# Rounding float64 weights to fp32: integer steps on ACT, DVE and GpSimd in place of identity products on PE

## The chip, the cores and the metric

The kernel runs on one core of a Trainium2 chip. Five instruction streams work side by side and meet only at semaphores: PE (matrix products), DVE (VectorE), ACT (ScalarE), POOL (GpSimd) and SP (which here only issues transfers). The metric is the device time of one execution in microseconds. The kernel before took 420.8 us in the median of three runs (420.77 to 421.42). A difference of about 0.2% (0.84 us) is what a measurement of this kernel can tell from no change.

## The reference

Per batch and head, 32 packed queries `p` attend over the keys and values, then the 576 queries `q` attend over the 32 packed rows. The result goes through a gated feed-forward layer. The three weights reach the kernel as float64; everything else is float32.

```python
def sm_attn(qq, kk, vv):
    s = scale * np.matmul(qq, kk.transpose(0, 1, 3, 2))
    s = s - np.max(s, axis=-1, keepdims=True)
    a = np.exp(s)
    a = a / (np.sum(a, axis=-1, keepdims=True) + 1e-09)
    return np.matmul(a, vv)
p_packed = sm_attn(p, k, v)            # 8 batches, 8 heads, 576 rows, 64 wide; 32 packed rows
x = sm_attn(q, p_packed, p_packed)     # then (8, 576, 512)
h = np.maximum(x @ w_in, 0.0)          # w_in 512 x 1024
conv_out += conv_w[k][None, None, :] * hp[:, k:k + S, :]   # 3 taps along the rows
gate = 1.0 / (1.0 + np.exp(-conv_out))
out = (h * gate @ w_out)               # w_out 1024 x 512
```

## The kernel before

The work is cut into sixteen attention groups (four heads of a batch each), eight batches of the feed-forward layer with eight column blocks j each, and 36 output tiles m of 128 rows.

- `attention(g)`: scores of the packed queries (PE L443), maximum and exponential (DVE L481, ACT L485), transposes on PE (L492) and copies out of PSUM on ACT (L495), the product with v (L501), then the second softmax on DVE (L525 to L555) with an exponential on ACT (L535).
- `packed_weight(b, hf)`: multiplies the packed values into half of `w_in` (L575), and splits the result into a high and a low part (ACT L587; the rest on DVE or on PE L591).
- `ffn1(b, j)`: twelve products in three part pairs (L627), ReLU and the middle tap on ACT (L639, L643), the other taps, a tanh and the gate (DVE L645, L649, L655, ACT L653). It writes one slice of `hgt`.
- `ffn2(m)`: splits an output tile's input into `xhi` (ACT L673) and `xlo` (DVE L676) and multiplies by `wo_hi` and `wo_lo` in 24 products (PE L692). The first of them, `ffn2(0)`, needs all eight slices of batch 0 and all four pieces of `w_out`. In the text its first product is called the **first output product**.
- `weight(i)`, i = 0 to 7: one megabyte of float64 weights each, four pieces of `w_in` and four of `w_out`. `f64_parts` turns the upper words into a truncated fp32 number (ACT L266, DVE L268, L270) and the lower words into a rest (DVE L272). PE adds the parts with products by an identity `ident` and its negative `minus` (L324), and ACT copies the sum out of PSUM (L328). For `w_out`, ACT also writes a high part `wo_hi` (L317), and the products give the rest.

The order of the instructions on each engine is a table, `ORDER`: two characters per step name the stream whose next step is issued. The class `Flow` carries a planner's costs along with it and puts filler products (`warm`, PE L242, products of `ident` with itself whose result nobody reads) into places where the planner sees PE idle, up to the first output product and not behind it. SP issues the transfers in the table's order through one queue; each `weight` loads into one of three buffers (`stage` and two parts of `hgt1`), which are reused once a piece has been read.

Of the kernel before, what the change touches and what calls it, by code (L numbers as in the profile page):

```python
# [49 lines left out]


# [11 lines left out]
class Flow:  # L63
# [10 lines left out]
    FILL_NS, FILL_COLS, MARGIN = 216, 512, 100  # L74

    LAG = {
        "PE": dict(PE=0, ACT=197, DVE=196, SP=200, POOL=200),
        "ACT": dict(PE=216, ACT=153, DVE=142, SP=200, POOL=200),
        "DVE": dict(PE=256, ACT=128, DVE=127, SP=200, POOL=200),
        "DATA": dict(PE=820, ACT=908, DVE=908, SP=0, POOL=0),  # L80
    }
# [103 lines left out]
def tile_packed_attention_conv_gate(  # L185
# [65 lines left out]
    def big():  # L251
        return ps.tile([128, 2, 512], F32, name="big", tag="big", bufs=3)
# [1 line left out]
    def small(tag="sm"):  # L254
        return ps.tile([128, 512], F32, name=tag, tag=tag)

    def f64_parts(tiles, raw, m, after=(), take=(), sets=None):

        pair = raw.rearrange("r (c t) -> r c t", t=2)
        up = pair[:, :, 1].bitcast(I32)  # L260
        low = pair[:, :, 0].bitcast(U32)
        yield Step("ACT", 93 + m * 14 // 15, after=after, take=take)
        t, e, rest = tiles()
        ti, ei = t.bitcast(I32), e.bitcast(I32)

        nc.scalar.activation(out=e, in_=up.bitcast(F32), func=AF.Prelu, scale=F64_REBIAS, alpha=-(2.0**32))  # L266
# [3 lines left out]
        nc.vector.tensor_scalar(out=ei, in0=ti, scalar1=-0x800000, scalar2=None, op0=ALU.bitwise_and)  # L270
        yield Step("DVE", 69 + m * 100 // 96, sets=sets)
        nc.vector.scalar_tensor_tensor(  # L272
            out=rest,
            in0=low,
            scalar=2.0**-52 if rest.dtype == F32 else -(2.0**-52),
            in1=e,
            op0=ALU.mult,
            op1=ALU.mult,
        )
# [17 lines left out]
    def weight(i):  # L297

        c, cols, src, st = weight_tile(i)
        hi, lo = (w[:, 2 * (i % 4) : 2 * (i % 4) + 2, :].rearrange("r c f -> r (c f)") for w in (wo_hi, wo_lo))  # L300
        token, tags = ("gw", ("ghi", "glo")) if i < 2 else ("x", ("xhi", "xlo"))
        parts = []

        def tiles():
            t, e = (wk.tile([128, DFF], F32, name="tmp", tag=tag) for tag in tags)
            parts.extend([(ident, t), (minus, lo)])
            return t, e, lo

        after = [("wd", i), "minus"] + ([("ws", i - 4)] if i >= 4 else [])
# [12 lines left out]
        for hf in range(2):
            for k, (w, x) in enumerate(parts):
                nc.tensor.matmul(  # L324
                    out=s[:, hf, :], lhsT=w, rhs=x[:, 512 * hf : 512 * hf + 512], start=k == 0, stop=k == len(parts) - 1
                )
        yield Step("ACT", 905, give=["big"], sets=[("w", i)])
        nc.scalar.copy(out=w_in_sb[:, c : c + 2, cols] if i < 4 else lo.rearrange("r (c f) -> r c f", c=2), in_=s)  # L328

    def conv_weight():  # L330
        src = conv_w.rearrange("k (j c) -> (k j) c", c=128)
# [1 line left out]
        st = [wk.tile([128, S], F32, name="s2", tag="s2") for _ in range(2)]  # L333
        if conv_w.dtype != F32:
            nc.gpsimd.dma_start(out=st[0][: 3 * NJ, :256].bitcast(I32), in_=src.bitcast(I32))
            t, e = st[1][: 3 * NJ, :128], st[1][: 3 * NJ, 128:256]
            yield from f64_parts(lambda: (t, e, e), st[0][: 3 * NJ, :256], 128)
            yield Step("DVE", 202)
            nc.vector.tensor_tensor(out=cw_raw, in0=t, in1=e, op=ALU.add)
# [414 lines left out]
```

## Time and profile before

| what | value |
|---|---|
| median of three runs | 420.8 us |
| span of the profiled execution | 418.8 us |
| what the runs have over the span | 2.0 us |
| PE instructions, DVE, ACT, POOL | 3343, 496, 440, 13 |
| HBM read and written | 37.77 MB, 9.44 MB |

The page gives the busy share of each engine over the whole span. Busy times of PE overlap from one product to the next, so a full PE is read from the chain of waits and from the list of what PE waited for, and not from its share alone. The span falls into three stretches: up to 29.3 us the first transfers set the pace, from there to 88.5 us the attention of the first groups, batch 0 of `ffn1` and the weights run together, and from the first output product on PE has a store of `ffn2` products to draw on.

### The profile page before, as it was taken

To read this page: it belongs to the slowest core of one execution; us is meant where nothing else is said; L and a number is where in the kernel's file an instruction comes from. 1 tells how busy PE (TensorE), PEld (TensorE's weight loads), DVE (VectorE), ACT (ScalarE), POOL (GpSimd) and SP (SyncE) were. 2 spreads that over 40 slices of the span, in tenths; PEclk is the share of its full clock that TensorE was granted. 3 is DMA by queue.
4 is the path that set the end of the run, shared out by engine and by line. 5 is a ranking of instruction groups with operands and counts; after the bars stand their busy time and mean duration, and the time that the engine had idled before them with its cause. 6 is when DMAs were issued, how large, how long until landed. Compare 5 with 4: busy or idle time off the path is not lost.

```text
span 418.8 us, 8142 instructions
## 1 busy us (share of the span) xinstructions
PE 409.3 (98%) x3343; PEld 324.7 (78%) x3343; DVE 346.7 (83%) x496; ACT 278.4 (66%) x440; POOL 1.6 (0%) x13
## 2 busy tenths in 40 slices
PE   6999999999999999999999999999999999999996
PEld 5755866689777878788868887888687878887884
DVE  2798999999999999899999999999857987766220
ACT  4789998986765676588656677766755567664221
POOL 1000000000000000000000000000000000000000
PEclk9999999999999999999999999999999999999999
DMA  8999997995646658014579223305000000010111
GB/s 267 391 356 287 153 255 196 166 178 108 134 89 140 132 123 154 2 52 84 125 174 175 60 74 84 55 27 109 27 25 26 27 25 27 25 52 0 52 75 50
DMA packets 141956, 47.73 MB, mean 114 GB/s; under 512 B 126036, under 2 KB 134228, under 8 KB 141920
## 3 DMA queue, kind: packets, MB, share of 16 engines
q1 hardware_dynamic: 141888, 47.20, 46.2%
q8 instruction: 26, 0.43, 0.4%
q14 instruction: 10, 0.08, 0.1%
q0 software_dynamic: 32, 0.02, 0.0%
HBM read 37.77 MB, written 9.44 MB: 113 GB/s over the span
## 4 chain that ended last, share of the span: by engine, by line
PE 91%; DMA 6%; ACT 1%; SPq 1%; issue 0%
PE fo L692 45%; PE big L627 25%; PE sm L692 4%; PE big L443 4%; DMA v<-in_v_dram 3%; PE big L575 3%; PE big L324 3%; PE sm L501 3%; DMA hgt<-in_moe_w_in_dram 2%; PE big L492 2%; PE idle L242 1%; PE big L427 1%; PE big L591 1%; ACT ghi L587 0%; SPq L463 0%; PE sm L517 0%
## 5 line engine op out<-in xcount | busy, mean ns | idle before, releaser
L692 PE MATMUL fo<-wo_hi,xhi 128*128 128x512 f32 x264 | 107.0, 405 | 0.7 <-ACT o L697 0.7
L692 PE MATMUL fo<-wo_hi,xlo 128*128 128x512 f32 x264 | 104.6, 396 | 0.0
L692 PE MATMUL fo<-wo_lo,xhi 128*128 128x512 f32 x264 | 104.5, 396 | 0.0
L692 PEld LDWEIGHTS fo<-wo_hi,xhi 128*128 128x128 f32 x264 | 49.7, 188 | 17.0 <-issue 4.1
L639 ACT ACTIVATE hbuf<-big 128x576 f32<-128x576 f32 x64 | 41.7, 653 | 31.7 <-PE big L627 29.9
L676 DVE TENSOR_TENSOR xlo<-hgt,xhi 128x1024 fp32r<-128x1024 f32 (+1 forms) x40 | 44.0, 1105 | 22.4 <-ACT xhi L673 22.2
L645 DVE SCALAR_TENSOR_TENSOR hgt<-hbuf,cw,hgt 128x576 f32<-128x576 f32 x64 | 51.4, 809 | 11.9 <-ACT hgt L643 11.4
L692 PEld LDWEIGHTS fo<-wo_hi,xlo 128*128 128x128 f32 x264 | 49.7, 188 | 12.0
L692 PEld LDWEIGHTS fo<-wo_lo,xhi 128*128 128x128 f32 x264 | 49.8, 189 | 9.6
L653 ACT ACTIVATE hgt<-hgt 128x576 f32<-128x576 f32 x64 | 43.4, 686 | 18.9 <-DVE hgt L649 18.8
L627 PE MATMUL big<-a2hi,ghi 128*128 128x288 f32 x256 | 55.9, 300 | 0.0
L627 PE MATMUL big<-a2hi,glo 128*128 128x288 f32 x256 | 54.6, 294 | 0.0
L627 PE MATMUL big<-a2lo,ghi 128*128 128x288 f32 x256 | 54.6, 294 | 0.0
L655 DVE SCALAR_TENSOR_TENSOR hgt<-hgt,hbuf 128x576 f32<-128x576 f32 x64 | 47.4, 746 | 7.3 <-ACT hgt L653 7.2
L649 DVE SCALAR_TENSOR_TENSOR hgt<-hbuf,cw,hgt 128x576 f32<-128x576 f32 x64 | 51.5, 812 | 0.9
L643 ACT ACTIVATE hgt<-hbuf,cw 128x576 f32<-128x576 f32 x64 | 49.0, 778 | 1.1
L697 ACT COPY o<-fo 128x512 f32<-128x512 f32 x33 | 19.3, 585 | 44.6 <-PE fo L692 42.0
L627 PEld LDWEIGHTS big<-a2hi,ghi 128*128 128x128 f32 x256 | 42.5, 188 | 7.0 <-ACT s L535 0.8
L673 ACT CAST xhi<-hgt 128x1024 fp32r<-128x1024 f32 (+1 forms) x40 | 38.0, 956 | 7.1 <-PE sm L692 3.9
L627 PEld LDWEIGHTS big<-a2lo,ghi 128*128 128x128 f32 x256 | 40.9, 188 | 0.0
L627 PEld LDWEIGHTS big<-a2hi,glo 128*128 128x128 f32 x256 | 40.9, 188 | 0.0
L501 PEld LDWEIGHTS sm<-v,a1T 128*32 128x32 f32 (+1 forms) x640 | 10.5, 108 | 9.0 <-issue 3.8
(90 smaller groups left out, 522.1 us busy)
## 6 DMA issues: line engine op xcount, KB each, us to landing
out_dram<-o SPq DMA_DIRECT2D x36, 256.0 KB, 2.2
v<-in_v_dram SPq DMA_DIRECT2D x16, 512.0 KB, 4.8
k<-in_k_dram SPq DMA_DIRECT2D x48, 144.0 KB, 3.6
q<-in_q_dram SPq DMA_DIRECT2D x48, 144.0 KB, 3.3
hgt<-in_moe_w_in_dram SPq DMA_DIRECT2D x3, 1024.0 KB, 9.3
hgt<-in_moe_w_out_dram SPq DMA_DIRECT2D x3, 1024.0 KB, 7.5
hgt<-in_k_dram SPq DMA_DIRECT2D x2, 576.0 KB, 5.1
hgt<-in_q_dram SPq DMA_DIRECT2D x2, 576.0 KB, 10.5
```

Of the source, the lines that this page charges most:

```text
L501: nc.tensor.matmul(out=t[32 * h : 32 * h + 32, :D], lhsT=a1T[r:, si, 32 * h : 32 * h + 32], rhs=G["v"][r:, head(g, h), si, :], start=si == ...
L627: nc.tensor.matmul(out=t[:, hf, :SH], lhsT=w[:, gg, js], rhs=x[:, hf * SH : (hf + 1) * SH], start=n == 0, stop=n == 3 * NG - 1,)
L639: nc.scalar.activation(out=h[:, 1 : S + 1].rearrange("c (f s) -> c f s", f=2), in_=t[:, :, :SH], func=AF.Relu, scale=0.5)
L643: nc.scalar.activation(out=d, in_=h[:, 1 : S + 1], func=AF.Copy, scale=cw[:, NJ + j : NJ + j + 1])
L645: nc.vector.scalar_tensor_tensor(out=d, in0=h[:, 0:S], scalar=cw[:, j : j + 1], in1=d, op0=ALU.mult, op1=ALU.add)
L649: nc.vector.scalar_tensor_tensor(out=d, in0=h[:, 2 : S + 2], scalar=cw[:, 2 * NJ + j : 2 * NJ + j + 1], in1=d, op0=ALU.mult, op1=ALU.add)
L653: nc.scalar.activation(out=d, in_=d, func=AF.Tanh)
L655: nc.vector.scalar_tensor_tensor(out=d, in0=d, scalar=1.0, in1=h[:, 1 : S + 1], op0=ALU.add, op1=ALU.mult)
L673: nc.scalar.copy(out=hi[:, :, o], in_=src)
L676: nc.vector.tensor_tensor(out=lo[:, :, o], in0=src, in1=hi[:, :, o].bitcast(F32), op=ALU.subtract)
L692: nc.tensor.matmul(out=t, lhsT=x[:, c, :], rhs=w[:, c, :], start=c + i == 0, stop=c == NJ - 1 and i == 2)
L697: nc.scalar.copy(out=o, in_=t)
```

## The change

`f64_parts` becomes `f64_rounded`. ACT rescales the upper word as before, and in a second pass reads the lower word and scales it to an integer of a few bits. DVE shifts the upper part by three bits; the truncating step and the product with the rest go. GpSimd adds the two as integers, so that the carry rounds the number. For `w_in` and the convolution weights that sum is the weight. For `w_out` ACT takes the high part from the sum and GpSimd subtracts it to get the low part. The products L324 and the copies L328 go. A weight's buffer counts as read after ACT's second pass, and no longer after DVE's product with the rest.

```diff
-    def f64_parts(tiles, raw, m, after=(), take=(), sets=None):
+    def f64_rounded(tiles, raw, m, after=(), take=(), give=(), read=None, sets=None):
...
         nc.scalar.activation(out=e, in_=up.bitcast(F32), func=AF.Prelu, scale=F64_REBIAS, alpha=-(2.0**32))
+        yield Step("ACT", 93 + m * 14 // 15, sets=read)
+
+        nc.scalar.activation(out=r.bitcast(I32), in_=low, func=AF.Copy, scale=2.0**-29)
         yield Step("DVE", 68 + m * 100 // 192)
-        nc.vector.tensor_scalar(out=ti, in0=ei, scalar1=3, scalar2=None, op0=ALU.logical_shift_left)
-        yield Step("DVE", 68 + m * 100 // 192)
-        nc.vector.tensor_scalar(out=ei, in0=ti, scalar1=-0x800000, scalar2=None, op0=ALU.bitwise_and)
-        yield Step("DVE", 69 + m * 100 // 96, sets=sets)
-        nc.vector.scalar_tensor_tensor(
-            out=rest,
-            in0=low,
-            scalar=2.0**-52 if rest.dtype == F32 else -(2.0**-52),
-            in1=e,
-            op0=ALU.mult,
-            op1=ALU.mult,
-        )
+        nc.vector.tensor_scalar(out=ei, in0=ei, scalar1=3, scalar2=None, op0=ALU.logical_shift_left)
+        yield Step("GP", 200 + m * 21 // 10, give=give, sets=sets)
+        nc.gpsimd.tensor_tensor(out=o.bitcast(I32), in0=ei, in1=r.bitcast(I32), op=ALU.add)
...
     def weight(i):
...
-        if i >= 4:
-            yield Step("ACT", 905)
-            nc.scalar.copy(out=hi, in_=parts[0][1])
-            parts.append((minus, hi))
-        ns = 2 * (864 + 234 * (len(parts) - 1))
-        yield Step("PE", ns, take=["big"], give=[token], sets=[("ws", i)], cols=2 * (1536 + 512 * len(parts)))
-        s = big()
-        for hf in range(2):
-            for k, (w, x) in enumerate(parts):
-                nc.tensor.matmul(
-                    out=s[:, hf, :], lhsT=w, rhs=x[:, 512 * hf : 512 * hf + 512], start=k == 0, stop=k == len(parts) - 1
-                )
-        yield Step("ACT", 905, give=["big"], sets=[("w", i)])
-        nc.scalar.copy(out=w_in_sb[:, c : c + 2, cols] if i < 4 else lo.rearrange("r (c f) -> r c f", c=2), in_=s)
+        if i < 4:
+            return
+        yield Step("ACT", 946)
+        nc.scalar.copy(out=hi, in_=src)
+        yield Step("GP", 2350, give=[token], sets=[("w", i)] + [("wp", i)] * (src is st))
+        nc.gpsimd.tensor_tensor(out=lo, in0=src, in1=hi.bitcast(F32), op=ALU.subtract)
...
     def conv_weight():
...
-            yield from f64_parts(lambda: (t, e, e), st[0][: 3 * NJ, :256], 128)
-            yield Step("DVE", 202)
-            nc.vector.tensor_tensor(out=cw_raw, in0=t, in1=e, op=ALU.add)
+            yield from f64_rounded(lambda: (e, r, cw_raw), st[0][: 3 * NJ, :256], 128)
```

The planner gets an engine `GP` with its own lags, and `ORDER` is a new table throughout (its first line is `"3400340363430303..."` in place of `"3400343436363436..."`). Three places show what that moves.

POOL, from its last setup instruction to its end; before, nothing followed there. `tmp_N` are the two parts of one piece of weights, `w_in_sb` and `wo_lo` the finished weights.

```order
masks.py:199 AFFINE_SELECT ident_64<-ident_64 128x128 [waits Pool_49]
L274 TENSOR_TENSOR cw_raw_71<-s2_90 24x128 [waits DVE_49,Activation_49]
L274 TENSOR_TENSOR w_in_sb_73<-tmp_294,tmp_295 128x2x512 [waits DVE_49,Activation_49]
L274 TENSOR_TENSOR w_in_sb_73<-tmp_369,tmp_370 128x2x512 [waits DVE_49,Activation_49]
L274 TENSOR_TENSOR w_in_sb_73<-tmp_223,tmp_224 128x2x512
L274 TENSOR_TENSOR tmp_441<-tmp_441,tmp_442 128x1024 [waits DVE_49,Activation_49]
L274 TENSOR_TENSOR w_in_sb_73<-tmp_537,tmp_538 128x2x512 [waits DVE_49,Activation_49]
L323 TENSOR_TENSOR wo_lo_75<-tmp_441,wo_hi_74 128x1024 [waits Activation_49]
```

Thirteen two-input instructions now stand on POOL, one small one and twelve of 1024 elements a partition (eight adds, four subtractions; the rows above show six, and the other six, for the last three pieces of `w_out`, follow them); all come before the first output product.

PE in the last third of the way to the first output product: before (`wo_hi`, `wo_lo`, `minus` are the parts of one `w_out` piece), then now.

```order
L443 MATMUL big_942<-kT_876,pT_615 32x288 x8
L242 MATMUL idle_960<-ident_64 128x128 x9
L324 MATMUL big_970<-tmp_817,ident_64 128x512
L324 MATMUL big_970<-wo_lo_75,minus_69 128x512
L324 MATMUL big_970<-wo_hi_74,minus_69 128x512
```

```order
L485 MATMUL big_925<-ident_64,a1_918 128x128 x5
L243 MATMUL idle_943<-ident_64 128x128 x20
L510 MATMUL sm_964<-ident_64,pb_941 128x128
L436 MATMUL big_966<-kT_912,pT_583 32x288 x8
L243 MATMUL idle_993<-ident_64 128x128 x3
L620 MATMUL big_997<-a2hi_436,ghi_685 128x288 x2
```

The identity products are gone and filler stands in their neighbourhood; in the whole program the filler calls go from 35 to 81, all ahead of the first output product.

ACT at the last piece of weights: before (`tmp_920` belongs to that piece; the `wo_hi` copy and the `wo_lo` copy out of PSUM), then now (`tmp_938` the upper words of the last piece, `tmp_939` its lower words).

```order
L317 CAST wo_hi_74<-tmp_920 128x1024
L639 ACTIVATE hbuf1_79<-big_1034 128x576
L653 ACTIVATE hgt0_76<-hgt0_76 128x576
L495 COPY a1T_1064<-big_1049 128x640
L553 CAST a2hi_1068<-a2t_1066 128x576
L512 ACTIVATE pb_1081<-sm_986,rs_951 128x128
L643 ACTIVATE hgt0_76<-hbuf1_79,cw_72 128x576
L653 ACTIVATE hgt0_76<-hgt0_76 128x576
L520 COPY ppT_1094<-sm_1092 128x128
L587 CAST ghi_1096<-big_1055 128x1024
L328 CAST wo_lo_75<-big_1071 128x1024
```

```order
L270 ACTIVATE tmp_939<-hgt1_77 128x1024
L636 ACTIVATE hgt0_76<-hbuf1_79,cw_72 128x576
L321 CAST wo_hi_74<-tmp_915 128x1024
L632 ACTIVATE hbuf0_78<-big_997 128x576
L588 CAST glo_848<-big_785 128x1024
L636 ACTIVATE hgt0_76<-hbuf0_78,cw_72 128x576
L513 COPY ppT_1047<-sm_964 128x128
L646 ACTIVATE hgt0_76<-hgt0_76 128x576
L321 CAST wo_hi_74<-tmp_938 128x1024
```

The `wo_hi` copy read a DVE result before and was followed by the copy of `wo_lo` out of PSUM; that copy is gone, and the `wo_hi` copy now stands eight instructions behind ACT's second pass over the same piece and reads GpSimd's sum.

More of the change, by code (lines that the diff above doesn't have):

```diff
@@ L47 @@
-    "6r6r6r6r6r6r6r6r5v5v6r5x5x5w6t6t6s6s6s6s6s6s6s6s6s6s6t6t6u6u6t6t6t6t6t6t6u6u6u6v6v6t6t6u6u6u6u6u6u6w6w6v6v6u6v6v"
-    "6v6v6v6v6v6x6v6w6w6w6w6w6w6w6r6w6w6w6x6x6x6x6x6x6x6x6x6x6x"
+    "343400033603030336023634070405050e0a043e043435340a0a0504010a06340534060c0h0c053c3f080c0h05050c053a3f053f0c050h05"
+    "0d3d0h050c3d0d050j0c050c0j050j090l0c3k3d050j053b0k0b0j0b3b0b050o0b3d050g0c0o3b0c0o0k0c0f3g050c3b3l0o373l0i053q0c"
+    "3q3f0s0j3l0c0c3q0i0n0c0j3q0c0c0m0i0i0j0c0j3h0q0j0q0c3s3l0q373t0j0j3u373h3l3s0r0q0j3h3h0v0j3t3s0z3t0j3s3t0r3u0x3t"
@@ L49 @@
+    "5n5l5n5m6o5n5n5m6o5n5m6o5n6o6o5q5r5s6p5q6p5q6p5s5q5s5s5s6p6p6p5s5r6p6p6p6n6p6q5q5p6p5s5r5p5t5t6q5p5t5q6q5t5t6q6q"
+    "6q5q6q5r6r5t6q5r5t5r6p6q5u6q6q5u6r5v5u6r5r5v6s5u5u6r6r6o6r5w6r5u5v6s5u5w5v5x6r5v5w6r5v5x5w5x6r6q5w5x6r6s5x6s6s6s"
+    "5x6s5v5x6s6s5w5w6s6t6s6t6t6t6u6t6t6t6t6t6t6s6u6v6v6u6u6u6u6u6u6t6u6t6u6v6w6u6v6v6v6v6v6w6v6u6v6r6v6x6w6w6w6x6w6w"
+    "6w6w6w6w6v6x6x6w6x6x6x6x6x6x6x6x"
 )
@@ L76 @@
     LAG = {
[L77 to L80, printed above, removed]
+        "PE": dict(PE=0, ACT=197, DVE=196, SP=200, POOL=200, GP=200),
+        "ACT": dict(PE=216, ACT=153, DVE=142, SP=200, POOL=200, GP=200),
+        "DVE": dict(PE=256, ACT=128, DVE=127, SP=200, POOL=200, GP=200),
+        "DATA": dict(PE=820, ACT=908, DVE=908, SP=0, POOL=0, GP=908),
+        "GP": dict(PE=300, ACT=250, DVE=250, SP=300, POOL=300, GP=200),
     }
@@ L87, in __init__ @@
         self.done = {}
-        self.free = dict(PE=4330.0, ACT=1900.0, DVE=600.0, SP=580.0, POOL=1350.0)
+        self.free = dict(PE=4330.0, ACT=1900.0, DVE=600.0, SP=580.0, POOL=1350.0, GP=2600.0)
         self.data = 4600.0
@@ L299, in weight @@
         c, cols, src, st = weight_tile(i)
-        hi, lo = (w[:, 2 * (i % 4) : 2 * (i % 4) + 2, :].rearrange("r c f -> r (c f)") for w in (wo_hi, wo_lo))
         token, tags = ("gw", ("ghi", "glo")) if i < 2 else ("x", ("xhi", "xlo"))
[L302 to L309, printed above, removed]
@@ L310, in weight, with tiles @@
-        if src.dtype != F32:
-            yield from f64_parts(tiles, st, DFF, after, [token], [("wp", i)])
+        after = [("wd", i)]
+        if i < 4:
+            dst = w_in_sb[:, c : c + 2, cols]
+            done = dict(give=[token], sets=[("w", i)])
+        else:
+            done = {}
+            hi, lo = (w[:, c : c + 2, :].rearrange("r c f -> r (c f)") for w in (wo_hi, wo_lo))
+        if src.dtype != F32:
+            t = []
+            def tiles():
+                t.extend(wk.tile([128, DFF], F32, name="tmp", tag=tag) for tag in tags)
+                return t[0], t[1], dst if i < 4 else t[0]
+            yield from f64_rounded(tiles, st, DFF, after, [token], read=[("wp", i)], **done)
+            src = t[0] if i >= 4 else None
+        elif i < 4:
+            yield Step("DVE", 1135, after=after, sets=[("wp", i), ("w", i)])
+            nc.vector.tensor_copy(out=dst, in_=st.rearrange("r (c f) -> r c f", c=2))
```

54 lines of the change are left out of this document (25 added, 29 removed).

## The prediction, made before the changed kernel ran

> **What bounds the kernel now.** I read the list of what PE waited for behind the first output product, then the chain of waits, then the stretches up to that product.
>
> ```profile
> PE fo L692 <- ACT o L697: 0.7, 1, 0.7
> ...
> 88.58 5.81 PE fo L692 x24
> ...
> 0.00:29.30 29.30, 25.21 (x228) 18.37 (x228) 17.52 (x33) 19.47 (x32) 1.59 (x13) 1.00 0.98 337
> 29.30:88.50 59.20, 58.22 (x705) 41.79 (x705) 56.88 (x88) 54.66 (x87) 0.00 (x0) 1.00 0.91 215
> 88.50:418.80 330.30, 325.84 (x2420) 264.51 (x2412) 272.35 (x377) 204.31 (x323) 0.00 (x0) 1.00 0.34 76
> ```
>
> The first row is the whole list of what PE waited for from 88.6 us on: once, 0.7 us. So the last 330.3 us are PE's own work, and they begin with the first output product at 88.5 us. Since the change leaves those products alone, its whole effect is how far it moves that moment. The three stretch rows (length, then busy time of PE, PEld, DVE, ACT, POOL, granted clock, DMA share) show why this isn't simple: from 29.3 to 88.5 us PE is busy for 58.2 of 59.2 us, but DVE is for 56.9, ACT for 54.7, and the transfers fill 91%. Four resources stand next to each other, and POOL is empty. The end is at (first output product) + 330.3, plus 2.0 us for what the median of 420.8 has over the span of 418.8.
>
> **PE: what goes.**
>
> ```profile
> 0.00:88.50 88.50, 21.10 (x56) 9.98 (x56) 1.00 0.94 255
> ...
> 34.52 2.85 PE big L324 x8
> ...
> 49.34 2.18 PE big L324 x6
> ...
> 68.47 2.20 PE idle L242 x18
> ```
>
> The first row is that of L324 alone: 56 records in 21.1 us, all ahead of the first output product. The chain has them as 2.85 us for an output piece and 2.18 for an input piece; four of each are 20.1, which I take. Filler costs 2.20 / 9 = 0.244 us a call (each call is two records), and 46 more calls are 11.2 us. They lie where the new order has nothing else for PE. So PE's sum to the first output product is 88.5 - 20.1 + 11.2 = 79.6 us, and PE would no longer be what sets it if another engine needs longer.
>
> ```profile
> 62.91 0.65 PE big L443 x16
> ...
> 64.41 1.79 PE big L627 x12
> ...
> 66.21 0.83 PE sm L501 x40
> ...
> 81.20 1.59 PE big L627 x12
> ```
>
> The new table also issues one score group (0.65) and one v product (0.83) behind the first output product that stood before it: 1.5 us more for PE afterwards, and as much less ahead of it (78.1). Between narrow and wide products it alternates four times less there; a wide group behind a narrow one takes 1.79 instead of 1.59, so 0.8 us less.
>
> **ACT: nothing goes.**
>
> ```profile
> L266 ACT ACTIVATE tmp<-hgt 128x1024 f32<-128x1024 f32 x6 | 7.0, 1161 | 0.7 <-DMA hgt<-in_moe_w_in_dram 0.7
> L328 ACT CAST wo_lo<-big 128x1024 fp32r<-128x1024 f32 x4 | 4.1, 1018 | 1.0 <-PE big L324 1.0
> L328 ACT COPY w_in_sb<-big 128x1024 f32<-128x1024 f32 x4 | 4.1, 1015 | 0.9 <-PE big L324 0.8
> ...
> L643 ACT ACTIVATE hgt<-hbuf,cw 128x576 f32<-128x576 f32 x11 | 8.5, 783 | 0.1
> L495 ACT COPY a1T<-big 128x640 f32<-128x640 f32 x7 | 4.9, 697 | 0.0
> L512 ACT ACTIVATE pb<-sm,rs 128x128 f32<-128x128 f32 x6 | 2.3, 381 | 0.4 <-PE sm L501 0.4
> L266 ACT ACTIVATE s<-s 24x128 f32<-24x128 f32 x1 | 0.3, 315 | 3.4 <-DMA s<-in_moe_conv_w_dram 3.4
> ```
>
> Eight copies of 1.02 us go (8.1) and eight second passes come. No row shows ACT turning an integer into an integer; L266 reads the same strided words, so 1.16 each or 9.3 (bounds: a plain copy's 1.02, and twice, 2.3, which would be 9 us more). The last four rows are one tap, one transposed copy and one scaling that the table moves behind the first output product (1.9 us), and a small second pass for the convolution weights that comes (0.3). ACT's sum, 19.5 + 54.7 = 74.1 us before (unrounded), becomes 73.7. What can shrink is its idle time, 14.4 us in the 88.5. Of this the list of waits gives PE as the releaser for 6.1, in seven rows of which these are the first and the last:
>
> ```profile
> ACT qT L433 <- PE big L427: 1.6, 2, 0.9
> ...
> ACT pb L512 <- PE sm L501: 0.4, 1, 0.4
> ```
>
> If all of it goes, ACT allows 88.5 - 0.4 - 6.1 = 82.0 us; if none, 88.1. I take 82.0, since PE has room now. New is ACT's wait for GpSimd's sum ahead of each `wo_hi` copy, with ReLU, tanh and casts queued behind it, for which PE and DVE wait. For the last piece eight instructions, some 5 us, stand between the pass and the copy; that hides one add, and I cost the wait at nothing. Without this cover it is the length of an add, four times.
>
> **DVE: what goes.**
>
> ```profile
> L272 DVE SCALAR_TENSOR_TENSOR wo_lo<-hgt,tmp 128x1024 fp32r<-128x1024 uint32 x6 | 7.2, 1204 | 0.1
> L270 DVE TENSOR_SCALAR tmp<-tmp 128x1024 int32<-128x1024 int32 x8 | 5.4, 678 | 0.1
> L272 DVE SCALAR_TENSOR_TENSOR s<-s,s 24x128 f32<-24x128 uint32 x1 | 0.3, 273 | 0.0
> L339 DVE TENSOR_TENSOR cw_raw<-s 24x128 f32<-24x128 f32 x1 | 0.3, 269 | 0.0
> L270 DVE TENSOR_SCALAR s<-s 24x128 int32<-24x128 int32 x1 | 0.2, 171 | 0.0
> L525 DVE STREAM_TRANSPOSE s<-big 128x576 f32<-128x576 f32 x4 | 3.1, 780 | 0.9 <-PE big L443 0.8
> L529 DVE TENSOR_REDUCE mx<-s 128x18 f32<-128x576 f32 x4 | 3.0, 740 | 0.1
> L416 DVE STREAM_TRANSPOSE kT<-k 128x1152 f32<-128x1152 f32 x4 | 5.4, 1360 | 0.0
> ```
>
> Eight products with the rest (1.20 us, 9.6) and eight truncations (0.68, 5.4) go, with 0.7 for the three small ones of the convolution weights. One `kT` transpose moves behind (1.36), one score transpose and one maximum move ahead (1.52). Net 15.5 us: 17.5 + 56.9 = 74.4 becomes 58.9. With DVE's idle time unchanged at 14.1, it allows 73.0 us, if GpSimd leaves it alone.
>
> **GpSimd: what comes.**
>
> ```profile
> masks.py:199 POOL TENSOR_SCALAR_AFFINE_SELECT ident<-ident 128x128 f32<-128x128 f32 x1 | 0.3, 315 | 0.1
> masks.py:197 POOL MEMSET ident<- 128x128 f32 x1 | 0.2, 205 | 0.3 <-POOLq L739 0.3
> L235 POOL MEMSET hbuf<- 128x1 f32 x3 | 0.2, 99 | 0.0
> ```
>
> No row shows a two-input GpSimd instruction. From 1 to 128 elements a fill grows by 0.83 ns an element and the select, which reads and computes, by 1.70. Over 1024 elements that is an estimate of 0.95 and 1.84 us; two inputs could double the select, 3.6. I take 1.84, the row nearest in kind. Twelve are 22 us (11 to 43) on an engine with 88 us to spare.
>
> The open question is whether they slow DVE, for which no row stands: POOL's work before is over ahead of DVE's first instruction. Two elementwise streams over the same memory may run untouched (0 us for DVE) or never together (all 22 us). I take the middle, 11 us. DVE then allows 73.0 + 11 = 84.0 us, ACT 82.0. In-order engines that hand work back and forth, two microseconds apart, each add waits to the other; I allow 0.8, half of the 1.6 by which ACT waited for DVE:
>
> ```profile
> ACT a2hi L553 <- DVE rs L563: 1.3, 1, 1.3
> ...
> ACT s L535 <- DVE s L531: 0.2, 1, 0.2
> ```
>
> Sum: 84.8 + 330.3 + 1.5 - 0.8 = 415.8 us of span, and **417.8 us** with the 2.0 around it, 0.7% faster. Of 20 us taken from PE some 3 remain.
>
> **The rivals.**
>
> *No hold-up.* DVE is free at 73.0 us, and ACT alone sets 82.0: 82.0 + 331.0 + 2.0 = 415.0 us; should ACT's waits for weight transfers (0.7 us in the row of L266 above, 1.4 for another piece) go too, 412.9. For it: DVE and ACT share 56.9 and 54.7 us of the same stretch without visible harm. Against: it needs four resources to run almost without gaps.
>
> *GpSimd holds DVE up for its whole length.* DVE allows 73.0 + 22 = 95.0 us: 428.0 us. The point from which it decides is 15.5 us of hold-up, 1.3 us for each of the twelve; from there the first output product is later than before. It strikes at the end of the second stretch, where the last three pieces put six GpSimd instructions among the taps of batch 0, of which most read two tiles in SBUF. For it: the DVE row of 56.9 in 59.2 us leaves no room. Against: part of DVE's work is transposes and maxima with one input, and there is slack early on.
> The Trainium skill, "SBUF — State Buffer", section "Who interferes with whom", says that a DVE instruction with two SBUF inputs, or in a two-port mode, and a GpSimd instruction that reads SBUF exclude each other: the second waits until the first has finished. By that rule the time lies between this rival and the forecast, as DVE's one-input instructions still run; no trace here shows it. The skill's "GPSIMD Engine Reference", section "Performance versus the Vector engine", gives 4497 ns for an add of 2048 elements, an estimate of 2.25 us here: 27 us for twelve and 433 us if every one of them blocked DVE.
>
> *The transfers decide.* 0.98 and 0.91 of the two stretches are busy with them, and the eight megabytes of weights are the same. If they hold the first output product where it is, the gain is nil: 88.5 gives 421.5 us. SP's queue now has two loads of keys and one of queries ahead of the first weights, and v ahead of the second; the buffers come free one DVE product earlier. Against: before, two groups of keys and one and a half of queries were fetched ahead that aren't needed by then.
>
> **How the numbers follow.** Forecast (415.6 to 420.6): 0.38. No hold-up (412.9 to 415.6): 0.24. Full hold-up (421.6 to 428): 0.30. Transfers (420 to 421.6): 0.08. Measurement can tell 0.2% here, 0.84 us. Faster means below 420.0: 0.24 and 0.31 of the forecast, 0.55. Same: 0.07 of the forecast and 0.08, less 0.01 at its upper edge: 0.14. Slower: 0.31. The range leaves out a tenth at each end: 412.5 (just below the lower value without hold-up) to 426.5 (some nine tenths of the full hold-up). The far ends, a second pass of twice the length and GpSimd at 3.6 us, lie in the tenth above.
>
> **What would show it.** First output product at 84.8 us (80 to 93), and 331 us behind it. L324 and L272's product gone, DVE busy for some 59 us plus hold-up ahead of it, ACT still for 74. The length of the twelve GpSimd rows: 1.84 us. If the taps (0.81 us) and additions of DVE keep their length while a GpSimd instruction runs, there is no hold-up; if their rows or the idle time ahead of them grow by a microsecond, there is. I would be wrong in kind if PE sets the moment after all, or if PE waits behind it.

## The result and the profile after

The changed kernel takes 430.5 us in the median of four runs (429.33 to 432.38), beside 420.8 us of four runs of the kernel before (420.77 to 421.42). The ratio is 1.0233, with a 95% interval of 1.0215 to 1.0252: 2.3% slower. The profiled execution took 429.33 us with a span of 427.6. The forecast was 417.8. One execution of the kernel before, in the last group of the experiments below, was in a slower state (571.42 us at a granted clock of 0.657) and stands in no comparison.

I read the profile in the same order as before. First the chain of waits: its row for the first output products (start, length, what).

```profile
97.66 5.60 PE fo L685 x24
```

Then the list of what PE waited for from 97.6 us on, which is one row, and the three stretches up to and from that product (length, then busy time of PE, PEld, DVE, ACT, POOL, granted clock, that is the share of its full clock that PE was given, and DMA share).

```profile
PE fo L685 <- ACT o L690: 0.7, 1, 0.7
```

```profile
0.00:29.30 29.30, 25.72 (x299) 20.59 (x300) 13.35 (x24) 21.16 (x38) 5.00 (x16) 1.00 0.99 346
29.30:97.60 68.30, 54.55 (x616) 42.78 (x615) 65.77 (x78) 51.58 (x79) 27.38 (x11) 0.90 0.80 179
97.60:427.60 330.00, 325.40 (x2469) 265.60 (x2467) 273.88 (x378) 206.71 (x327) 0.00 (x0) 1.00 0.34 77
```

The last stretch is as long as before, 330.0 us, and PE still waits once in it. So the whole loss lies ahead of the first output product, which moved from 88.5 to 97.6 us. In the second stretch PE is now busy for 54.6 of 68.3 us and ACT for 51.6; DVE is for 65.8. DVE sets the moment, although the change takes instructions away from it. The new POOL work is there, and it is longer than estimated; its groups (busy time, mean ns of one):

```profile
L274 POOL TENSOR_TENSOR tmp<-tmp 128x1024 int32<-128x1024 int32 x4 | 10.3, 2584 | 22.0 <-DVE sm L533 14.4 <-DVE tmp L272 7.6
L323 POOL TENSOR_TENSOR wo_lo<-tmp,wo_hi 128x1024 fp32r<-128x1024 f32 x4 | 10.1, 2519 | 5.5 <-ACT wo_hi L321 5.5
L274 POOL TENSOR_TENSOR w_in_sb<-tmp 128x1024 int32<-128x1024 int32 x4 | 10.0, 2507 | 22.9 <-DVE sm L533 13.2 <-DVE tmp L272 9.7
```

And DVE's own groups up to 97.6 us have long instructions (the lengths without GpSimd come with the first experiment):

```profile
L648 DVE SCALAR_TENSOR_TENSOR hgt<-hgt,hbuf 128x576 f32<-128x576 f32 x8 | 11.2, 1410 | 0.0
L638 DVE SCALAR_TENSOR_TENSOR hgt<-hbuf,cw,hgt 128x576 f32<-128x576 f32 x9 | 10.5, 1177 | 1.5 <-ACT hgt L636 1.5
L642 DVE SCALAR_TENSOR_TENSOR hgt<-hbuf,cw,hgt 128x576 f32<-128x576 f32 x8 | 8.3, 1050 | 0.0
L537 DVE TENSOR_TENSOR s<-s,sm 128x576 f32<-128x576 f32 x4 | 7.0, 1750 | 0.1
L548 DVE TENSOR_TENSOR a2lo<-a2t,a2hi 128x576 fp32r<-128x576 f32 x4 | 5.2, 1296 | 0.1
...
L524 DVE TENSOR_TENSOR s<-s,mx 128x576 f32<-128x576 f32 x4 | 3.8, 946 | 0.1
...
L542 DVE STREAM_TRANSPOSE a2t<-s 128x576 f32<-128x576 f32 x4 | 3.1, 772 | 0.1
L531 DVE TENSOR_REDUCE sm<-s 128x18 f32<-128x576 f32 x4 | 3.0, 738 | 0.0
L533 DVE TENSOR_SCALAR sm<-sm 128x18 f32<-128x18 f32 x4 | 2.3, 585 | 0.0
```

A gate (L648) takes 1410 ns in the mean, a normalization (L537) 1750. The transposes and the reductions, which have one input, keep their 772 and 738 ns. In order of time, near the end of the second stretch, the timeline of both engines (start, length, instruction) shows why:

```profile
81.34 2.77 POOL L274 TENSOR_TENSOR tmp<-tmp 128x1024 int32<-128x1024 int32 x1 [2.70 <-DVE tmp L272]
81.79 2.94 DVE L638 SCALAR_TENSOR_TENSOR hgt<-hbuf,cw,hgt 128x576 f32<-128x576 f32 x1
84.07 2.86 POOL L323 TENSOR_TENSOR wo_lo<-tmp,wo_hi 128x1024 fp32r<-128x1024 f32 x1
84.77 2.78 DVE L642 SCALAR_TENSOR_TENSOR hgt<-hbuf,cw,hgt 128x576 f32<-128x576 f32 x1
87.47 1.37 DVE L409 STREAM_TRANSPOSE qT<-q 128x1152 f32<-128x1152 f32 x1
...
89.27 2.47 POOL L323 TENSOR_TENSOR wo_lo<-tmp,wo_hi 128x1024 fp32r<-128x1024 f32 x1 [2.35 <-ACT wo_hi L321]
89.45 2.91 DVE L648 SCALAR_TENSOR_TENSOR hgt<-hgt,hbuf 128x576 f32<-128x576 f32 x1
```

The tap at 81.79 begins while GpSimd adds. It ends at 84.73, 0.62 us behind the end of the add at 84.11. The subtraction that GpSimd begins at 84.07 ends at 86.93, and the next tap 0.62 us behind that. The time that DVE stands shows as a longer instruction and not as idle time, so DVE reads as full. The tanh behind the second tap (ACT L646) waited 4.79 us for it.

### The profile page after: what moved, and what is told of

It is laid out like the page before. It is cut to its first block, busy times and chain, and to the rows that moved or that the text cites. A ratio compares the mean times of both kernels' runs of the same rounds, so it can differ in the third digit from the quotient of the medians.

```text
span 427.6 us, 8191 instructions
## 1 busy us (share of the span) xinstructions
PE 405.7 (95%) x3379; PEld 329.0 (77%) x3379; DVE 353.0 (83%) x477; ACT 279.4 (65%) x441; POOL 32.4 (8%) x26
## 4 chain that ended last, share of the span: by engine, by line
PE 83%; DVE 9%; DMA 3%; ACT 2%; issue 1%; SPq 1%; POOL 0%; POOLq 0%; DVEq 0%; ACTq 0%
PE fo L685 44%; PE big L620 22%; PE sm L685 4%; PE big L436 3%; PE big L568 3%; DMA q<-in_q_dram 3%; PE sm L494 2%; DVE hgt L648 2%; DVE hgt L638 2%; PE big L485 1%; PE big L420 1%; PE idle L243 1%; DVE hgt L642 1%; DVE s L537 1%; ACT ghi L580 1%
## 5 line engine op out<-in xcount | busy, mean ns | idle before, releaser
L638 DVE SCALAR_TENSOR_TENSOR hgt<-hbuf,cw,hgt 128x576 f32<-128x576 f32 x64 | 55.0, 860 | 14.9 <-ACT hgt L636 14.5
L646 ACT ACTIVATE hgt<-hgt 128x576 f32<-128x576 f32 x64 | 43.5, 685 | 28.1 <-DVE hgt L642 28.0
L620 PE MATMUL big<-a2hi,ghi 128*128 128x288 f32 x256 | 57.8, 308 | 0.0
L620 PE MATMUL big<-a2lo,ghi 128*128 128x288 f32 x256 | 56.0, 301 | 0.0
L620 PE MATMUL big<-a2hi,glo 128*128 128x288 f32 x256 | 55.9, 300 | 0.0
L648 DVE SCALAR_TENSOR_TENSOR hgt<-hgt,hbuf 128x576 f32<-128x576 f32 x64 | 52.7, 829 | 3.3 <-ACT hgt L646 2.8
L642 DVE SCALAR_TENSOR_TENSOR hgt<-hbuf,cw,hgt 128x576 f32<-128x576 f32 x64 | 53.8, 844 | 1.1
L620 PEld LDWEIGHTS big<-a2hi,ghi 128*128 128x128 f32 x256 | 44.0, 194 | 8.5 <-issue 0.9
L620 PEld LDWEIGHTS big<-a2lo,ghi 128*128 128x128 f32 x256 | 42.3, 194 | 0.0
L620 PEld LDWEIGHTS big<-a2hi,glo 128*128 128x128 f32 x256 | 42.2, 194 | 0.0
L243 PE MATMUL idle<-ident 128*128 128x128 f32 x162 | 23.3, 293 | 2.5 <-POOL ident masks.py:199 2.5
```

The costliest lines, as they stand in the source:

```text
L243: nc.tensor.matmul(out=t[:, :128], lhsT=ident, rhs=ident, start=True, stop=True)
L620: nc.tensor.matmul(out=t[:, hf, :SH], lhsT=w[:, gg, js], rhs=x[:, hf * SH : (hf + 1) * SH], start=n == 0, stop=n == 3 * NG - 1,)
L638: nc.vector.scalar_tensor_tensor(out=d, in0=h[:, 0:S], scalar=cw[:, j : j + 1], in1=d, op0=ALU.mult, op1=ALU.add)
L642: nc.vector.scalar_tensor_tensor(out=d, in0=h[:, 2 : S + 2], scalar=cw[:, 2 * NJ + j : 2 * NJ + j + 1], in1=d, op0=ALU.mult, op1=ALU.add)
L646: nc.scalar.activation(out=d, in_=d, func=AF.Tanh)
L648: nc.vector.scalar_tensor_tensor(out=d, in0=d, scalar=1.0, in1=h[:, 1 : S + 1], op0=ALU.add, op1=ALU.mult)
```

## The experiments

Unless a run says otherwise, each is one execution. The runs came in three groups, each beside the kernel before on the same chip: it took 420.71 us and 421.36 us in single executions of the first two, and 420.72 to 422.83 us in ten of the third. By their times alone, single runs that differ by one or two microseconds can't be told apart; the moment of the first output product and the lengths of the rows in the traces say more. Line numbers shift by a few between the edited kernels.

**GpSimd's instructions cut to eight columns.** The order table stays; the rest of the sums and differences is left out, and ACT writes the destinations in its second pass.

```diff
-        nc.gpsimd.tensor_tensor(out=o.bitcast(I32), in0=ei, in1=r.bitcast(I32), op=ALU.add)
+            nc.gpsimd.tensor_tensor(out=o[:, :8].bitcast(I32), in0=ei[:, :8], in1=ei[:, 8:16], op=ALU.add)
...
-        nc.gpsimd.tensor_tensor(out=lo, in0=src, in1=hi.bitcast(F32), op=ALU.subtract)
+        nc.gpsimd.tensor_tensor(out=lo[:, :8], in0=src[:, :8], in1=hi[:, :8].bitcast(F32), op=ALU.subtract)
```

> Leaves out: the integer add and the subtraction for all but 8 of 1024 columns; ACT's second pass writes the weights' places instead, so that every instruction, its order, its filler and its waits stay and only the twelve GpSimd instructions shrink. Theory 'exclusion' (GpSimd's reads of two tiles stop DVE instructions with two SBUF inputs; 19 us of stretched DVE rows ahead of the first output product): DVE's taps and additions go back to 0.75 to 0.81 us, the first output product comes at 78 to 84 us instead of 97.4, the span is 408 to 415. Rival 'order' (the new table, its filler and the fallen clock make the first stretch long by themselves): taps may shrink, but the first output product stays behind 90 us and the span above 420.

It took 413.6 us, with the first output product at 81.90. DVE's groups of this run:

```profile
L643 DVE SCALAR_TENSOR_TENSOR hgt<-hbuf,cw,hgt 128x576 f32<-128x576 f32 x12 | 9.5, 798 | 0.0
L647 DVE SCALAR_TENSOR_TENSOR hgt<-hbuf,cw,hgt 128x576 f32<-128x576 f32 x11 | 8.8, 809 | 0.1
L653 DVE SCALAR_TENSOR_TENSOR hgt<-hgt,hbuf 128x576 f32<-128x576 f32 x11 | 8.1, 746 | 0.5 <-ACT hgt L651 0.4
...
L529 DVE TENSOR_TENSOR s<-s,mx 128x576 f32<-128x576 f32 x5 | 3.8, 755 | 0.1
L542 DVE TENSOR_TENSOR s<-s,sm 128x576 f32<-128x576 f32 x5 | 3.7, 743 | 0.1
...
L553 DVE TENSOR_TENSOR a2lo<-a2t,a2hi 128x576 fp32r<-128x576 f32 x4 | 3.0, 752 | 0.1
...
L538 DVE TENSOR_SCALAR sm<-sm 128x18 f32<-128x18 f32 x5 | 0.9, 173 | 0.1
```

These are the lengths without GpSimd. The difference of each group's mean, times its count in the changed kernel, is the hold-up there: 8 x 0.664 = 5.3 for the gates, 9 x 0.379 + 8 x 0.241 = 5.3 for the taps, 4 x 1.007 = 4.0 for L537, 2.2 for L548, 0.8 for L524, 1.6 for L533: **19.3 us**, of 30.4 us that the twelve GpSimd instructions took. The new order by itself is good: with GpSimd out of the way it gains 7 us. ACT now stands nearest to setting the product: it idles for 1.3 us of the second stretch, DVE for 3.5. That stretch (columns as above):

```profile
29.30:81.90 52.60, 51.09 (x622) 40.33 (x623) 49.12 (x78) 51.29 (x80) 3.67 (x9) 1.00 0.95 220
```

**GpSimd writes only.** Eight columns again, and three fills over each whole destination, which overwrite the weights.

```diff
+            for _ in range(3):
+                nc.gpsimd.memset(o, 0.03)
...
+        for _ in range(3):
+            nc.gpsimd.memset(lo.bitcast(F32), 0.0)
```

> Leaves out: as above; behind each 8-column add or subtraction GpSimd fills the whole destination three times (write only; about 1 us each, so about as long as the 2.5 us of an add). 'Exclusion by reads': DVE instructions with two SBUF inputs keep 0.75 to 0.81 us, only the two-port shift (L272 of the changed kernel, 0.68) may wait; span 408 to 416. Rival 'any GpSimd traffic slows DVE': taps stretch as in the changed kernel, to 1.05 to 1.4 us on average ahead of the first output product; span 423 to 430. 'Order': above 420 with taps of normal length.

414.5 us, product at 82.66. GpSimd's three groups of fills and two DVE groups of this run:

```profile
L280 POOL MEMSET w_in_sb<- 128x1024 f32 x12 | 12.3, 1024 | 0.7
L331 POOL MEMSET wo_lo<- 128x1024 f32 x12 | 12.0, 1002 | 0.7
L280 POOL MEMSET tmp<- 128x1024 f32 x12 | 11.4, 954 | 0.7
```

```profile
L656 DVE SCALAR_TENSOR_TENSOR hgt<-hgt,hbuf 128x576 f32<-128x576 f32 x11 | 8.1, 746 | 0.9 <-ACT hgt L654 0.9
...
L272 DVE TENSOR_SCALAR tmp<-tmp 128x1024 int32<-128x1024 int32 x8 | 5.9, 739 | 0.1
```

35.7 us of GpSimd work, more than in the changed kernel, and the gate still takes 746 ns. GpSimd's writes don't hold up DVE's instructions with two inputs. They do touch those with one input and a scalar: the shift L272 takes 739 ns in the mean instead of 682 (1.01 us once), the addition on 128x18 elements 271 instead of 173. That is some 0.9 us in sum, and the product comes 0.8 us later than with the short instructions.

**GpSimd reads one operand.** Eight columns, and two copies per piece in place of the fills; the weights are again overwritten.

```diff
+            for _ in range(2):
+                nc.gpsimd.tensor_copy(out=o if len(o.shape) == 3 else r, in_=e.rearrange("r (c f) -> r c f", c=2) if len(o.shape) == 3 else e)
...
+        for _ in range(2):
+            nc.gpsimd.tensor_copy(out=lo, in_=src)
```

> Leaves out: as above; behind each 8-column add or subtraction GpSimd copies one 1024-column tile twice (one input read, one written; 0.9 to 1.3 us each). 'Exclusion by reads, whatever their number': taps are stretched to about 1.0 to 1.4 us on average and the span is 418 to 428. Rival 'only two-input GpSimd instructions exclude': taps at 0.75 to 0.81, span 408 to 416.

422.7 us, product at 90.50. One group of GpSimd and one of DVE:

```profile
L331 POOL CAST wo_lo<-tmp 128x1024 fp32r<-128x1024 f32 x8 | 11.5, 1438 | 0.5
```

```profile
L656 DVE SCALAR_TENSOR_TENSOR hgt<-hgt,hbuf 128x576 f32<-128x576 f32 x9 | 9.3, 1040 | 0.0
```

With 30.7 us of copies, about what the twelve adds and subtractions took, the gates are at 1040 ns and the product 8.6 us later than without GpSimd (90.50 - 81.90). One read is enough. The copies are shorter, so a DVE instruction that meets one stands for less long.

**GpSimd's twelve instructions on DVE.** The places in the table stay.

```diff
-        nc.gpsimd.tensor_tensor(out=o.bitcast(I32), in0=ei, in1=r.bitcast(I32), op=ALU.add)
+        nc.vector.tensor_tensor(out=o.bitcast(I32), in0=ei, in1=r.bitcast(I32), op=ALU.add)
...
-        nc.gpsimd.tensor_tensor(out=lo, in0=src, in1=hi.bitcast(F32), op=ALU.subtract)
+        nc.vector.tensor_tensor(out=lo, in0=src, in1=hi.bitcast(F32), op=ALU.subtract)
```

> Computes the adds on DVE, which adds in fp32 and not in exact integers, and the subtractions on DVE too, at the same places of the same table; PE, ACT and SP are unchanged word for word, and GpSimd has nothing. 'Exclusion': the 19 us of hold-up go and twelve DVE instructions of 1.2 us come (14.5 us), so the first output product moves from 97.4 to about 93 and the span from 427.6 to about 423 (420 to 425). 'Order': no change or later, 427 and more.

424.8 us, product at 91.94, taps and gates at 0.74 to 0.81 us. An add or subtraction takes 1.21 us on DVE (14.5 for twelve); the trace shows the adds as custom instructions over 2048 halves of 16 bits. So the work costs DVE less when DVE does it than the 19.3 us that it stands when GpSimd does it.

**The same interference in the kernel before.** Four short adds of GpSimd behind each piece of weights, into a tile that nobody reads.

```diff
+        for n in range(4):
+            if i < 4:
+                a = b = w_in_sb[:, c + n // 2, cols][:, 256 * (n % 2) : 256 * (n % 2) + 256]
+            else:
+                a, b = (x.bitcast(F32)[:, 256 * n : 256 * n + 256] for x in (hi, lo))
+            nc.gpsimd.tensor_tensor(out=scratch, in0=a, in1=b, op=ALU.add)
```

> The kernel before, with its order table and its identity products, and behind each piece of weights four more GpSimd adds of 256 columns into a tile that nobody reads (some 0.75 us each, 3 us a piece, 24 us in all). No other engine waits for them but the next writer of what they read. Theory (reads by GpSimd exclude DVE's two-input instructions): DVE's two-input rows ahead of the first output product grow by 10 to 19 us in sum, and as DVE was busy for 56.9 of the 59.2 us before it, the product comes 7 to 14 us later, 428 to 435 us. Rival (it was the new order, not GpSimd, that made the kernel slower): 420.8 us, rows unchanged.

427.5 us beside 421.4, product at 95.06 instead of 88.58: the old order is hurt too, a little less than expected (6.5 us, not 7 to 14). DVE is busy for 81.9 us up to that product (74.4 before), so 7.5 us longer, not 10 to 19. The 32 short adds took 31.6 us on GpSimd, but one takes only 0.99 us, and the longest hold-up of a DVE instruction in this trace is some 0.6 us. Two DVE groups of this run:

```profile
L271 DVE TENSOR_SCALAR tmp<-tmp 128x1024 int32<-128x1024 int32 x8 | 6.3, 784 | 0.1
...
L551 DVE TENSOR_TENSOR s<-s,sm 128x576 f32<-128x576 f32 x4 | 4.5, 1120 | 0.0
```

The normalization (L551) takes 1120 ns instead of 751, and the truncation (L271), which has one input and a scalar, 784 instead of 678. By the same account as above, the instructions with two inputs grow by 5.8 us in sum, those with one input and a scalar by 2.1.

**The clock.** The granted clock falls to 0.70 and 0.85 in two slices of the changed kernel, in or behind places where PE waits (3.5 us for ACT ahead of the first, 5.0 us in the second). 38 more filler calls go there.

```diff
+        warm({2: 13, 4: 18}.get(g, 0))
         t = score(ppT, G["qT"], g, range(HG))
...
+        if (b, hf) == (1, 1):
+            warm(7)
```

> The changed kernel with 38 more filler products at three places where PE waits and the granted clock then falls to 0.70 to 0.85: 13 ahead of the q scores of group 2, 18 ahead of those of group 4, 7 ahead of the second half of the packed weight of batch 1. Theory (the hold-up on DVE sets the moment, the dips of the clock are only what PE's waits leave behind): within 1 us of 430.5, even with the clock up. Rival (the dips lengthen the twelve-product groups, 5.37 for 3.17 us and 3.0 for 1.58, and that is on the path): 2 to 4 us earlier, 426.5 to 428.5.

431.1 us, product at 99.45. The first fence has three slices of the changed kernel, the second those of this run (columns as in the stretches above):

```profile
40.00:50.00 10.00, 9.48 (x74) 7.93 (x75) 8.27 (x12) 8.32 (x14) 4.75 (x2) 0.70 0.99 245
80.00:90.00 10.00, 3.90 (x76) 2.65 (x84) 9.96 (x8) 5.21 (x9) 6.31 (x3) 0.85 0.10 16
90.00:97.60 7.60, 6.95 (x48) 5.68 (x37) 7.09 (x8) 4.94 (x9) 1.74 (x1) 0.75 0.49 78
```

```profile
40.00:50.00 10.00, 9.13 (x96) 7.40 (x102) 9.87 (x14) 9.49 (x16) 4.28 (x2) 1.00 1.02 223
80.00:90.00 10.00, 9.11 (x115) 7.54 (x113) 9.96 (x9) 5.19 (x9) 6.05 (x3) 1.00 0.16 24
90.00:99.40 9.40, 6.91 (x48) 5.96 (x49) 8.89 (x11) 5.72 (x10) 2.05 (x1) 0.82 0.40 65
```

The first two dips are gone and nothing is gained. Behind the first, two taps of DVE (L638, here L641) begin 1.1 us earlier but take 4.17 us beside GpSimd instead of 2.84, and DVE's 9.96 of 10 us in the second slice are the same. The product even comes 1.8 us later, and the end of the chain of waits shows where from (start, length, what; the changed kernel first):

```profile
94.76 0.73 PE big L584 x2
95.49 1.59 PE big L620 x12
```

```profile
95.06 1.22 PE big L587 x2
96.28 2.59 PE big L623 x12
```

But for five transposes these are the last products of PE ahead of the first output product. In the changed kernel the granted clock is back at 1.00 over them, so the third dip, which ends before, isn't on the path. In this run they begin 0.3 us later, behind a wait of 2.4 us for ACT, and the clock is 0.56 over them: 3.81 us for 2.32, the other 1.5 us. So the clock doesn't explain why the changed kernel is slower, but a dip that falls on the last products costs some 1.5 us.

**Without GpSimd and without the carry.** ACT's second pass truncates to three bits, and one DVE instruction shifts the upper part and puts the bits in. The weights are truncated to fp32 and not rounded.

```diff
-        nc.scalar.activation(out=r.bitcast(I32), in_=low, func=AF.Copy, scale=2.0**-29)
+        nc.scalar.activation(out=r.bitcast(I32), in_=low, func=AF.Copy, scale=2.0**-29 - 2.0**-39, bias=-0.4995)
-        nc.vector.tensor_scalar(out=ei, in0=ei, scalar1=3, scalar2=None, op0=ALU.logical_shift_left)
+        nc.vector.scalar_tensor_tensor(out=o.bitcast(I32), in0=ei, scalar=3, in1=r.bitcast(I32), op0=ALU.logical_shift_left, op1=ALU.bitwise_or)
-        nc.gpsimd.tensor_tensor(out=o.bitcast(I32), in0=ei, in1=r.bitcast(I32), op=ALU.add)
...
-        nc.gpsimd.tensor_tensor(out=lo, in0=src, in1=hi.bitcast(F32), op=ALU.subtract)
+        nc.vector.tensor_tensor(out=lo, in0=src, in1=hi.bitcast(F32), op=ALU.subtract)
```

> The changed kernel with its order table, without GpSimd on the weights: ACT's second pass takes the top three bits of the lower word by truncation (a scale and a bias), so no carry is needed, and one two-input DVE instruction shifts the upper part and puts the bits in, in place of the shift and of GpSimd's add. The four subtractions run on DVE. The weights are truncated to fp32 instead of rounded. Against the run with all adds and subtractions on DVE (424.8 us, first output product at 91.9) DVE loses eight adds of 1.2 us and its eight shifts grow from 0.68 to 1.2 us: 5.4 us less. Theory (what delays the first output product is the DVE time that the rounding takes, as work or as hold-up): product at 86 to 88, 418.5 to 421.5 us, taps at 0.74 to 0.81 us. Rival (the new order on PE and ACT sets the moment once GpSimd's queue is there): no better than 424.

418.3 us, product at 85.53, both just below what was expected. Its two stretches up to the product:

```profile
0.00:29.30 29.30, 23.51 (x274) 18.68 (x274) 11.36 (x22) 19.74 (x35) 1.58 (x13) 1.00 0.99 336
29.30:85.50 56.20, 52.49 (x638) 40.68 (x639) 55.71 (x82) 52.23 (x81) 0.00 (x0) 1.00 0.96 219
```

DVE idles 0.5 us in the second stretch and 17.9 in the first.

> The kernel with truncation on ACT and DVE and with the subtractions on DVE, again, timed against the kernel before: one look gave 418.3 against 421.4 us. Theory: 418 to 419 us, ratio 0.992 to 0.996, so faster than both kernels. If the one look was luck: 420 to 422.

The same kernel timed against the kernel before: 417.6 us (417.35 to 418.23, six runs), ratio **0.9914**, 95% interval 0.9896 to 0.9932, both a little below what was expected; its product came at 85.26. It is 0.9% faster than the kernel before, and so faster than both kernels, though its weights are only truncated.

**The four subtractions back on GpSimd.** The kernel with truncation, without its last edit.

> As the run with truncation on ACT and DVE, but the four subtractions stay on GpSimd, which then runs four full-length instructions in place of twelve. Theory (each two-input GpSimd instruction costs DVE's stream some 1.6 us, 19.3 / 12): hold-up 6.4 us against 4.8 us of DVE work for the same subtractions, so 0 to 3 us later than that run; taps of batch 0 lengthen only beside those four. Rival (only a dense sequence of GpSimd work holds DVE, four alone find gaps): 3 to 5 us earlier than that run.

422.9 us, product at 90.62. Up to it the taps and gates are 6.4 us longer (10.3, 9.2 and 8.0 us for 10, 9 and 8 instructions that take 0.797, 0.809 and 0.738 otherwise), just 4 x 1.6. But the product came 5.1 us later where 0 to 3 were expected and the rival had it earlier. The hold-up strikes the taps and the gate ahead of the last block of `ffn1`, two of the four within the last 16 us; when DVE does the subtractions, two of them stand behind the last of those taps, and no tanh waits for them. And the last twelve products of `ffn1` then took 2.88 us instead of some 1.6, with the granted clock at 0.56 from 86.2 to 90.0 us: 1.3 of the 5.1 us are the clock's, as in the run with more filler.

**DVE work in the first and in the second stretch.** Twelve additions of 320 columns that nobody needs, in the kernel with truncation: six each behind two early instructions, or two each behind six gates of batch 0.

```diff
+    def extra(n):
+        for _ in range(n):
+            nc.vector.tensor_tensor(out=scratch, in0=scratch, in1=scratch, op=ALU.add)
```

> The same kernel with twelve additions of 320 columns on DVE (some 0.42 us each, 5 us in sum) into a tile that nobody reads, in the first stretch: six behind the first reciprocal of the sums and six behind the second maximum, where DVE waits 2.8 us each for PE. Theory (DVE has 16 to 18 us of idle time in the first stretch, which the transfers set, so DVE work there is free, and work taken away there gains nothing): first output product within 0.7 us of 85.5, 418 to 419.5 us. Rival (DVE's bound is work plus a fixed idle time, as the prediction had it): 5 us later, 423.

> The same twelve additions in the second stretch, two behind the gate of each of six column blocks of batch 0. Theory (DVE idles 0.5 of 56 us there and sets the first output product): 4.5 to 5.5 us later, product at 90 to 91, 423 to 424 us. Rival (ACT or PE set it next to DVE and give way): under 2 us later.

Early: 417.6 us, product at 85.31. Late: 423.8 us, product at 91.50, a little later than expected. The additions took 5.9 and 5.8 us. The two stretches of each run, early first:

```profile
0.00:29.30 29.30, 24.67 (x291) 19.21 (x291) 17.80 (x34) 20.56 (x37) 1.80 (x14) 1.00 0.99 338
29.30:85.30 56.00, 52.15 (x630) 40.51 (x623) 55.05 (x82) 51.13 (x79) 0.00 (x0) 1.00 0.97 217
```

```profile
0.00:29.30 29.30, 24.37 (x274) 19.12 (x274) 11.11 (x21) 19.09 (x34) 1.81 (x14) 0.94 0.98 339
29.30:91.50 62.20, 54.14 (x641) 42.07 (x640) 61.31 (x94) 52.99 (x82) 0.00 (x0) 0.97 0.88 199
```

In the first stretch DVE's busy time grows from 11.4 to 17.8 us and the product stays (85.31, beside 85.53 and 85.26 without them). In the second it grows from 55.7 to 61.3 and the product is 6.0 us later.

## Why the prediction was wrong

The frame held. The end is the first output product plus 330 us (331.0 taken, 330.0 measured), PE no longer sets that moment (80.3 us busy up to it; 79.6 taken, or 78.1 without the two groups that move behind it), and DVE with GpSimd's hold-up does. ACT's bound of 82.0 us is what remains once GpSimd is out of the way: 81.90 with the instructions cut short. That it fits so well is in part luck, for ACT was busy for 72.0 us and idle for 9.9 there, where 73.7 and 8.3 were taken. That run's 413.6 us lies in the rival's 412.9 to 415.6. ACT's second passes took 1.16 to 1.17 us, as taken. ACT's wait for GpSimd's sum, costed at nothing, is not among its waits. The transfers did not hold the product at 88.5: it came at 81.90 with the same loads.

The step that failed is DVE's bound, 58.9 us of work + 14.1 of idle time + 11 of hold-up = 84.0. Measured up to 97.6 us: 13.35 + 65.77 = 79.1 busy, of which 19.3 hold-up and 59.8 work, and 18.5 idle.

- **The hold-up was 19.3 us, not 11.** I took the middle between nothing and 22 because no row showed the two engines side by side. It is 1.6 us for each of the twelve instructions; the rival put the break-even at 1.3. It was mis-sized twice. A GpSimd instruction takes 2.5 us in the mean and 2.36 to 2.38 where it was there first (the two at 64.3 and 69.9 us), not 1.84: the row of the small select, extended by its length, gave too little. And 63% of that time falls on DVE, not half.
- **DVE's idle time grew by 4.4 us** where I left it at 14.1. In the first stretch it went from 11.8 to 16.0 us (29.3 less the busy time). The products and truncations that the change takes from DVE there, ahead of transfers that set the pace, leave a gap and nothing else. The two runs with extra additions show it from the other side: 5.9 us of DVE work there cost nothing, 5.8 us behind it cost 6.0. So of the 15.5 us that I credited to DVE, only those in the second stretch counted.
- Work was 0.9 us above the sum, and the 0.8 for mutual waits doesn't come on top where DVE never idles: 8.3 + 4.4 + 0.9 - 0.8 = 12.8, from 84.8 to 97.6.

Against the kernel before, DVE's account up to the product reads: work 74.4 to 59.8 (-14.6), idle 14.1 to 18.5 (+4.4), hold-up +19.3, together the 9.1 us of delay. With the idle time right, the break-even was a hold-up of 88.5 - 59.8 - 18.5 = 10.2 us and not 15.5; the 11 us that I took would already have meant slower.

The rival of full hold-up named the mechanism and the place (the taps of batch 0 beside the last six GpSimd instructions), and forecast 428.0. It came nearest, but not by its own sum: it took 22 us of hold-up, more than the 19.3 measured, and idle time as before. The rule of the Trainium skill, "SBUF — State Buffer", section "Who interferes with whom", is borne out: DVE instructions with two inputs in SBUF and GpSimd instructions that read exclude each other (2.94 us for a tap of 0.80), fills that only write leave the gate at 746 ns, and one-input transposes and reductions go on. I had the rule beside the sum, read from it a time between the forecast and 428.0, and gave that rival 0.30; it should have had most of the chance. Not all one-input instructions went on: the small addition with a scalar (L533) took 585 ns instead of 173. The estimate of 2.25 us from the skill's "GPSIMD Engine Reference", section "Performance versus the Vector engine", was nearer than my 1.84, and 0.1 us short of the 2.36 measured.

## What to carry to other kernels

Moving elementwise work from DVE's neighbours to an idle GpSimd is not free where DVE is full: count, for every GpSimd instruction that reads SBUF, the DVE instructions beside it that have two inputs or one and a scalar, and compare that with doing the work on DVE itself (here 19.3 against 14.5 us, and 9.1 with the carry avoided: 0.54 more for each of eight shifts and 1.21 for each of four subtractions). A hold-up shows as longer instructions and not as idle time, so compare an operation's mean length before and after. And when work is taken from an engine, ask stretch by stretch whether that engine sets the pace there; time freed ahead of a transfer is idle time.

## What the runs showed of the hardware

- GpSimd took about 1.0 us to fill 1024 fp32 elements a partition, 1.14 to 1.44 us to copy or cast them, and 2.35 to 2.40 us to add two operands undisturbed. Only the kinds that read lengthened DVE's instructions with two inputs.
- A DVE instruction with one input and a scalar on 128x18 elements took 173 ns alone, 585 in the mean beside GpSimd's adds and 271 beside its fills; it was held up as well, while transposes and reductions were not.
- GpSimd was held up in turn: 2.47 to 2.86 us for an instruction of the changed kernel that met one of DVE with two inputs, 2.35 to 2.40 otherwise.
- The granted clock fell to 0.70 to 0.85 in or behind places where PE waited; filler kept it at 1.00 in two of them and the product came no earlier. A dip on the last products ahead of the first output product cost 1.5 us.
